# Loads of a Fourier-mixing kernel: 128 partitions in place of 112

## The chip, the cores and the metric

The kernel runs on one core of a Trainium2 chip. Five engines work beside each other: TensorE (PE, with its weight loads as PEld), VectorE (DVE), ScalarE (ACT), GpSimd (POOL) and SyncE (SP), which here only issues DMA transfers. Each engine takes its instructions in the order of the program and waits for others by semaphores. DRAM is reached through 16 DMA engines. The metric is device time in microseconds (us).

## What is computed

x has the shape (8, 3136, 256). Each batch is convolved circularly with a filter along its 3136 tokens, then mixed by a two-dimensional Fourier transform, and goes through a normalised two-layer product:

```
X = np.fft.rfft(x, axis=1);  Y = X * (filt_r + 1j * filt_i)
y = np.fft.irfft(Y, n=3136, axis=1)
u = y + np.real(np.fft.fft(np.fft.fft(y, axis=1), axis=2))
un = (u - mean(u)) / sqrt(var(u) + 1e-6)
out = u + np.maximum(un @ w_ch1, 0) @ w_ch2
```

## The kernel before

The transform over 3136 = 112 x 28 tokens is done in stages of small matrix products, which is why 112 rows stand in most tiles. For each of the eight batches a chain runs:

- `forward1`: seven loads of x, `[112, 4, 256]` in float32 each (448 KB), from the caller's array of the shape (8, 112, 28, 256). VectorE takes the largest magnitude of each tile (`absmax`, the tile `mx`), a power of two `sx` comes of the seven, then 14 steps each scale a piece, multiply it by the table `s1`, split it in two float16 halves (`ast`, four buffers) and write it to the DRAM scratch tensor `d1`. Batch 0 has its own version, `first_forward1`, which multiplies in float32 while x still arrives.
- `forward2`: seven loads `at` of `[112, 8, 256]` float16, from d1 in another order of rows (runs of 512 bytes), 448 KB each. Their products with the table `s2` are multiplied by the filter, folded into the ring `eo` for the second transform, turned round by DMA transposes (`z`; on PE in batch 0), multiplied by the table `i1` and written to a second scratch tensor, `d2`.
- `inverse2` (the batch's `back` part): seven loads `b` of d2, like those of d1, products with the table `i2`, and stores `ys` to a third tensor, `dy`.

Groups of 256 rows of dy are then fetched as `y`, mixed (`channels`), normalised (`un`, `u16`), turned by two DMA transposes into `ut`, and multiplied by both weights in eight parts: `first_product` (tile `h`, line 770; ScalarE and VectorE make its two halves in lines 779 and 780) and `second_product` (`acc`, line 799). These two products of the weights are the larger part of PE's work. Batch b + 1's chain is woven between the groups of batch b.

d1 and d2 are allocated anew for each batch from a pool with two buffers each. All tables are loaded once, s2 and i1 in chunks behind the at loads of batch 0.

What sets the order: the generators `there` and `back` are advanced step by step from a loop over PE's products, `after(...)` adds marks before which an instruction is not put, and a scheduler with a timeline of its own then sets the order on each engine. All DMAs stand in SP's one queue. They use eight semaphores in turn, so that a DMA is not issued before the one eight places ahead of it has landed.

The lines that matter, and the allocation of the scratch:

```
nc.sync.dma_start(xs[q], a["x"][b, :, 4 * q : 4 * q + 4])
d1v = d1.rearrange("(u r) n h c -> (r n h) u c", r=2)
last = nc.sync.dma_start(ats[ch], d1v[:, 8 * ch : 8 * ch + 8])
d1 = dp.tile([112, 28, 2, 256], F16, tag="d1", name=f"d1_{b}")
```

Of the kernel before, what the change touches and what calls it, by code (L numbers as in the profile page):

```python
# [9 lines left out]
F32 = mybir.dt.float32  # L10
F16 = mybir.dt.float16
# [13 lines left out]
C = 256  # L25
# [169 lines left out]
def _program(ctx, tc, nc, a, NB):  # L195
    cp = ctx.enter_context(tc.tile_pool(name="cp", bufs=1))
    xp = ctx.enter_context(tc.tile_pool(name="xp", bufs=7))
    fp = ctx.enter_context(tc.tile_pool(name="fp", bufs=2))
    mp = ctx.enter_context(tc.tile_pool(name="mp", bufs=2))
    tp = ctx.enter_context(tc.tile_pool(name="tp", bufs=2))  # L200
    dp = ctx.enter_context(tc.tile_pool(name="dp", bufs=2, space=DRAM))
# [4 lines left out]
    marks = {}  # L206
# [15 lines left out]

    s1 = cp.tile([112, 2, 112], F16, name="s1")
    s1f = fp.tile([112, 112], F32, tag="t2", name="s1f", bufs=2)
    s2 = cp.tile([112, 56, 2, 56], F16, name="s2")
    i1 = cp.tile([112, 28, 2, 112], F16, name="i1")
    i2 = cp.tile([112, 2, 2, 2, 64], F16, name="i2")
# [102 lines left out]

    def first_forward1(d1):

        xs = [xp.tile([112, 4, 256], F32, tag="big", name=f"x_0_{q}") for q in range(7)]
        m = tp.tile([112, 8], F32, tag="mx", name="mx_0")
        ps = {}

        def product(q):
            if q in (3, 4):
                p = ps_o.tile([128, 2, 256], F32, tag="pso", name=f"s1_0_{q}")[:112]
            else:  # L340
                p = bank(f"s1_0_{q}")[:112].rearrange("p (n c) -> p n c", c=256)
# [17 lines left out]
        yield  # L359
        for q in range(14):  # L360
            if q not in ps:
                product(q)
            p = ps.pop(q)
            st = fp.tile([112, 2, 2, 256], F16, tag="ast", name=f"ast_0_{q}", bufs=4)
            marks["act"] = nc.scalar.activation(st[:, :, 0], p, AF.Copy, scale=sx[:112, 1:2]).ins
            marks["dve", q] = nc.vector.scalar_tensor_tensor(
                st[:, :, 1], p, sx[:112, 1:2], st[:, :, 0], op0=ALU.mult, op1=ALU.subtract
            ).ins
            marks["d1", q] = nc.sync.dma_start(d1[:, 2 * q : 2 * q + 2], st).ins
            yield  # L370

    def forward1(b, d1):
        xs = [xp.tile([112, 4, 256], F32, tag="big", name=f"x_{b}_{q}") for q in range(7)]
        m = tp.tile([112, 8], F32, tag="mx", name=f"mx_{b}")
        for q in range(7 + XLAG):
            with after(("y", 1), ("un", 0)) if b == 1 else nullcontext():
                if q < 7:
                    with after("sp") if b > 1 else nullcontext():
                        nc.sync.dma_start(xs[q], a["x"][b, :, 4 * q : 4 * q + 4])
                if q >= XLAG:  # L380
                    with after("h"):
                        absmax(m[:, q - XLAG : q - XLAG + 1], xs[q - XLAG], AX.XY)
            if q < 6 + XLAG:
                yield
        nc.vector.tensor_reduce(m[:, 7:8], m[:, 0:7], axis=AX.X, op=ALU.max)
        row = pow2(m[:, 7:8], f"x{b}")
        sx = tp.tile([128, 2], F32, tag="sx", name=f"sx_{b}", bufs=3)
        spread(sx, row, f"x{b}")
        sxs[b] = sx
        yield  # L390
        for q in range(14):
            x = xs[q // 2][:, 2 * (q % 2) : 2 * (q % 2) + 2]
            x16 = fp.tile([112, 2, 2, 256], F16, tag="x16", name=f"x16_{b}_{q}", bufs=3)
            nc.scalar.activation(x16[:, 0], x, AF.Copy, scale=sx[:112, 1:2])  # L394
            nc.vector.scalar_tensor_tensor(
                x16[:, 1], x, sx[:112, 1:2], x16[:, 0], op0=ALU.mult, op1=ALU.subtract
            )
            p = bank(f"s1_{b}_{q}")[:112].rearrange("p (n c) -> p n c", c=256)
            for i, (hs, hx) in enumerate(((0, 0), (0, 1), (1, 0))):
                nc.tensor.matmul(p, s1[:, hs], x16[:, hx], start=i == 0, stop=i == 2)  # L400
            st = fp.tile([112, 2, 2, 256], F16, tag="ast", name=f"ast_{b}_{q}", bufs=4)
            nc.scalar.copy(st[:, :, 0], p)
            nc.vector.tensor_tensor(st[:, :, 1], p, st[:, :, 0], op=ALU.subtract)
            nc.sync.dma_start(d1[:, 2 * q : 2 * q + 2], st)
            yield

    def load_s2(ch):
        nc.sync.dma_start(s2[:, 8 * ch : 8 * ch + 8], a["c_s2"][:, 8 * ch : 8 * ch + 8])

    def load_i1(ch):  # L410
        nc.sync.dma_start(i1[:, 4 * ch : 4 * ch + 4], a["c_i1"][:, 4 * ch : 4 * ch + 4])

    def forward2(b, d1, d2):
        al = cp.tile([128, 3], F32, name=f"alpha_{b}")
# [94 lines left out]
        def inverse1(ch, h):  # L509
# [33 lines left out]
    def inverse2(b, d2):  # L543
        dy = dp.tile([2, NS, 256], F32, tag="dy", name=f"dy_{b}", bufs=3)
        dys[b] = dy
        d2v = d2.rearrange("(m r) j l c -> (r j l) m c", r=2)
        al = alphas[b]
        bts = {}

        def load(c):  # L550
            if c < 7:
                bts[c] = fp.tile([112, 4, 2, 256], F16, tag="b2", name=f"b2_{b}_{c}", bufs=2)
                with after("dy"):
                    marks["b", c] = marks["sp"] = nc.sync.dma_start(
                        bts[c].rearrange("p j h c -> p (j h) c"), d2v[:, 8 * c : 8 * c + 8]
                    ).ins

        def store(k, s, r, ys, c, j0):
# [383 lines left out]
    for r, f in enumerate(("frT", "fiT")):  # L942
        for h in range(4):
            part = slice(784 * (h % 2), 784 * (h % 2) + 784)
            nc.sync.dma_start(ft[:, r, h // 2, part], a[f][:, h // 2, part])
    nc.sync.dma_start(fnyq, a["frN"])
    for q in range(14):
        advance(9 + q)
        if q == 2:
            with after(("d1", 0)):  # L950
                nc.sync.dma_start(s2[:, :16], a["c_s2"][:, :16])
        for i in range(8):
            if FILTERS_AT[i] == q:
                measure_filters(i)
        weigh(9 + q)
# [40 lines left out]
def device_arrays(x, filt_r, filt_i, moe_w_ch1, moe_w_ch2):  # L996
# [22 lines left out]


# [27 lines left out]
```

## Time and profile before

| | |
|---|---|
| median of 3 runs | 1541.23 us |
| the three runs | 1541.23, 1531.26, 1541.39 us |
| span of the profiled execution, first to last instruction | 1534.0 us |
| PE busy in the span | 91% |
| HBM read, written | 113.36 MB, 102.76 MB |
| DMA packets' time on the hardware queue, share of 16 engines | 72.5% |

Of the profiled execution the page gives the span alone, not a time of the kind that the runs have.

A profile is one execution. Busy time of an engine is the time of its instructions; a wait is the idle time just before an instruction, put down to what came last before it ("DVE mx L267 <- DMA x<-x" is VectorE idle ahead of line 267, until an x load landed). A busy share averages over stages with different limits, so the stretches of the span are read one by one. The kernel's time is that of the chain that ends last; work on other engines counts only where that chain waits for it. Names like `at<-d` say what is written and what is read.

### The profile page before, as it was taken

How to read it: one execution, taken by the hardware profiler on the slowest of the kernel's cores; microseconds unless marked ns; L12 is line 12 of the kernel's file. 1: busy time of each engine (PE TensorE's matmuls, PEld its weight loads, DVE VectorE, ACT ScalarE, POOL GpSimd, SP SyncE). 2: the span in 40 equal slices, each digit the busy share in tenths (PEclk: the TensorE clock that was granted, in tenths of full speed). 3: DMA queues.
4: the chain of work that ended last, by engine and by line, in shares of the span. 5: the costliest groups of instructions: out<-in, count | busy, mean ns of one | idle time of the engine just before them, and what ended most of it. 6: DMA issues, size and time to landing. Idle time of an engine off the chain costs nothing.

```text
span 1534.0 us, 30300 instructions
## 1 busy us (share of the span) xinstructions
PE 1398.7 (91%) x11331; PEld 934.1 (61%) x11331; DVE 1092.8 (71%) x2388; ACT 771.3 (50%) x1426; POOL 539.9 (35%) x682
## 2 busy tenths in 40 slices
PE   5454899787999999999999999899999999999998
PEld 1432567454665677566765677566665667666666
DVE  5576878586967887687758877688767877565562
ACT  4466545354545464474544654374644655443341
POOL 3652049205810195006720284016620284110110
PEclk8675999998999999999999999999999999999999
DMA  8868478959985797859986796859876896644320
GB/s 263 218 205 219 101 163 176 219 157 206 203 216 146 175 227 174 208 152 214 192 192 161 192 231 159 211 146 220 183 189 158 195 237 144 166 107 110 95 55 29
DMA packets 429491, 268.98 MB, mean 175 GB/s; under 512 B 218624, under 2 KB 395824, under 8 KB 429344
## 3 DMA queue, kind: packets, MB, share of 16 engines
q1 hardware_dynamic: 429344, 267.05, 72.5%
q8 instruction: 89, 1.46, 0.4%
q14 instruction: 58, 0.48, 0.1%
HBM read 113.36 MB, written 102.76 MB: 141 GB/s over the span
## 4 chain that ended last, share of the span: by engine, by line
PE 67%; DMA 11%; DVE 7%; issue 3%; POOL 3%; ACT 2%; SPq 1%; DVEq 0%; POOLq 0%; ACTq 0%
PE h L770 26%; PE acc L799 26%; DMA x<-x 3%; PE s L400 3%; PE y L577 3%; DMA at<-d 2%; PE mix L646 2%; DVE y L656 2%; PE i L514 1%; DMA b<-d 1%; PE i L516 1%; PE i L515 1%; PE s L449 1%; DVE mx L267 1%; PE s L450 1%
## 5 line engine op out<-in xcount | busy, mean ns | idle before, releaser
L770 PE MATMUL h<-ut,w1s 128*128 128x512 f16 x2352 | 590.8, 385 | 24.6 <-DVE h L780 20.5
L799 PE MATMUL acc<-w2s,h 128*128 128x256 f16 x4704 | 599.9, 274 | 1.3 <-DVE h L780 1.3
L799 PEld LDWEIGHTS <-h 128*128 128x128 f16 x4704 | 456.4, 98 | 146.8 <-issue 13.6
L779 ACT ACTIVATE h<-h 128x512 f16<-128x512 f32 x392 | 233.1, 595 | 411.9 <-PE h L770 404.6
L780 DVE SCALAR_TENSOR_TENSOR h<-h,h 128x512 f16<-128x512 f32 x392 | 267.6, 683 | 200.3 <-ACT h L779 199.3
L741 POOL TENSOR_TENSOR u<-un,u 128x512 f16<-128x512 f32 x94 | 107.8, 1163 | 758.0 <-ACT u L739 745.6
L770 PEld LDWEIGHTS <-w1s 128*128 128x128 f16 x2352 | 223.8, 99 | 236.7 <-issue 48.1
L656 DVE SCALAR_TENSOR_TENSOR y<-mix,alpha,y 128x508 f32<-128x508 f32 (+1 forms) x368 | 156.0, 474 | 8.2 <-PE mix L646 6.9
L736 ACT ACTIVATE un<-y,sb 128x256 f32<-128x256 f32 x196 | 101.8, 589 | 44.0 <-DVE sb L729 38.8
L469 POOL TENSOR_TENSOR y<-yt,y 128x448 f16<-128x448 f32 x105 | 108.4, 1036 | 16.5 <-ACT y L468 16.2
L584 ACT ACTIVATE ys<-y,alpha 128x512 f32<-128x512 f32 x112 | 76.1, 686 | 71.4 <-PE y L577 71.0
L519 DVE TENSOR_TENSOR bt<-i,bt 112x512 f16<-112x512 f32 x112 | 75.7, 682 | 49.1 <-ACT bt L518 47.4
L267 DVE TENSOR_REDUCE mx<-x 112x1 f32<-112x1024 f32 x56 | 67.7, 1214 | 52.0 <-DMA x<-x 52.0
L463 POOL TENSOR_TENSOR yt<-yt,t 128x224 f32<-128x224 f32 x112 | 73.9, 660 | 81.9 <-DVE t L459 53.6
L455 DVE SCALAR_TENSOR_TENSOR yt<-s,pF,ft 128x448 f32<-128x448 f32 x112 | 75.3, 675 | 37.7 <-PE s L450 34.9
L449 PE MATMUL s<-s,at 112*128 112x56 f16 x896 | 62.7, 191 | 32.6 <-DMA at<-d 28.1
L400 PE MATMUL s<-x,s 112*112 112x512 f16 x294 | 87.3, 388 | 3.9 <-ACT x L394 1.9
L577 PE MATMUL y<-b,i 112*64 112x512 f16 (+1 forms) x480 | 74.1, 396 | 18.1 <-DMA b<-d 17.9
L518 ACT CAST bt<-i 112x512 f16<-112x512 f32 x112 | 64.9, 585 | 49.9 <-PE i L516 43.7
L808 DVE SCALAR_TENSOR_TENSOR y<-acc,beta,y 128x512 f32<-128x512 f32 x98 | 71.2, 742 | 25.7 <-PE acc L799 25.5
L468 ACT CAST y<-yt 128x448 f16<-128x448 f32 x112 | 62.6, 564 | 38.6 <-POOL yt L464 35.6
L449 PEld LDWEIGHTS <-at 112*128 112x128 f16 x896 | 55.8, 98 | 42.6 <-DMA at<-d 36.0
(133 smaller groups left out, 1663.4 us busy)
## 6 DMA issues: line engine op xcount, KB each, us to landing
x<-x SPq DMA_DIRECT2D x56, 448.0 KB
d<-ast SPq DMA_DIRECT2D x112, 224.0 KB
at<-d SPq DMA_DIRECT2D x56, 448.0 KB
d<-bt SPq DMA_DIRECT2D x112, 224.0 KB
b<-d SPq DMA_DIRECT2D x56, 448.0 KB
out<-y SPq DMA_DIRECT2D x98, 256.0 KB
y<-dy SPq DMA_DIRECT2D x92, 256.0 KB
dy<-ys SPq DMA_DIRECT2D x208, 112.0 KB
```

Source lines behind the costliest of these rows:

```text
L267: nc.vector.tensor_reduce(dst, src, axis=axis, op=ALU.max, apply_absolute_value=True)
L400: nc.tensor.matmul(p, s1[:, hs], x16[:, hx], start=i == 0, stop=i == 2)
L449: nc.tensor.matmul(o, w, s2[:, U, 0].rearrange("p (r k) -> p r k", r=2), start=True, stop=False)
L469: last = half(b, hf == 1).tensor_tensor(ylo, ytv, yhi, op=ALU.subtract)
L577: nc.tensor.matmul(p[64 * h : 64 * h + 64, js], i2[:, t, h, i], bt[:, o + js.start : o + js.stop, h], start=i == 0, stop=i == 1,)
L656: nc.vector.scalar_tensor_tensor(out, p, al, y, op0=ALU.mult, op1=ALU.add)
L736: nc.scalar.activation(un[:m, k], y[:m, t, k], AF.Identity, bias=sb[:m, i, 1:2], scale=sb[:m, i, 3:4])
L741: marks["u16", g] = low.tensor_tensor(u16[:m, :, :, 1], unv, u16[:m, :, :, 0], op=ALU.subtract).ins
L770: marks["pe"] = nc.tensor.matmul(p[:, c0 : c0 + n].rearrange("p (t k q) -> p t k q", k=2, q=m), w1s[:, d, hw, 128 * f : 128 * f + 128], ut ...
L779: nc.scalar.activation(h[:, 0, :nt], p[:, :nt], AF.Relu)
L780: marks["h"] = nc.vector.scalar_tensor_tensor(h[:, 1, :nt], p[:, :nt], 0.0, h[:, 0, :nt], op0=ALU.max, op1=ALU.subtract).ins
L799: nc.tensor.matmul(acc[:m, k], h[:, hh, c0 : c0 + m], w2s[:, f, hw], start=f == 0 and k == 0 and i == 0, stop=f == 7 and k == 1 and i == 2,)
```

## The change

Loads of x, of d1, of d2 and of the tables s2, i1 and i2 fill 128 partitions in place of 112. Compute instructions still use the first 112: `xs`, `ats`, `bts`, `s2`, `i1` and `i2` are now views `[:112]` of larger tiles, and the stores to d1 and d2 still have 112 rows. An SBUF tile takes as many bytes in each partition as before.

- x comes padded with 16 rows of zeros, as (8, 7, 128, 4, 256): each tile is one contiguous piece of 512 KB.
- The tables get 16 rows of zeros; a chunk of s2 or i1 grows from 196 to 224 KB.
- d1 and d2 get a 113th row, and there are two of each for the whole run (`scratch`, used by even and odd batches). A load reads 128 rows from the same start: the last 16 are the first rows of the next slot, and for the last slot the tail, which is filled with zeros once. Loads from d1 and d2 grow from 448 to 512 KB.

```diff
+    def rows128(d, u0, n):
+        v = d[:112].rearrange("(u r) n h c -> (r n h) u c", r=2)[:, u0 : u0 + n]
+        (row, _), *rest = v.ap
+        return bass.AP(tensor=v.tensor, offset=v.offset, ap=[[row, 128], *([s, m] for s, m in rest)])
...
-    s2 = cp.tile([112, 56, 2, 56], F16, name="s2")
+    s2_rows = cp.tile([128, 56, 2, 56], F16, name="s2")
+    s2 = s2_rows[:112]
...
-        xs = [xp.tile([112, 4, 256], F32, tag="big", name=f"x_{b}_{q}") for q in range(7)]
+        raw = [xp.tile([128, 4, 256], F32, tag="big", name=f"x_{b}_{q}") for q in range(7)]
+        xs = [t[:112] for t in raw]
...
-                        nc.sync.dma_start(xs[q], a["x"][b, :, 4 * q : 4 * q + 4])
+                        nc.sync.dma_start(raw[q], a["x"][b, q])
...
-            nc.sync.dma_start(d1[:, 2 * q : 2 * q + 2], st)
+            nc.sync.dma_start(d1[:112, 2 * q : 2 * q + 2], st)
...
-                ats[ch] = xp.tile([112, 8, 256], F16, tag="big", name=f"at_{b}_{ch}")
-                last = nc.sync.dma_start(ats[ch], d1v[:, 8 * ch : 8 * ch + 8])
+                at = xp.tile([128, 8, 256], F16, tag="big", name=f"at_{b}_{ch}")
+                ats[ch] = at[:112]
+                last = nc.sync.dma_start(at, rows128(d1, 8 * ch, 8))
...
-                bts[c] = fp.tile([112, 4, 2, 256], F16, tag="b2", name=f"b2_{b}_{c}", bufs=2)
+                bt = fp.tile([128, 4, 2, 256], F16, tag="b2", name=f"b2_{b}_{c}", bufs=2)
+                bts[c] = bt[:112]
...
-                        bts[c].rearrange("p j h c -> p (j h) c"), d2v[:, 8 * c : 8 * c + 8]
+                        bt.rearrange("p j h c -> p (j h) c"), rows128(d2, 8 * c, 8)
...
+    scratch = [
+        [dp.tile([113, 28, 2, 256], F16, tag=f"d{i}_{k}", name=f"d{i}_{k}", bufs=1) for i in (1, 2)] for k in range(2)
+    ]
+    zeros = fp.tile([16, 256], F16, tag="ef", name="zeros", bufs=1)
+    nc.vector.memset(zeros, 0.0)
+    def fill_tails():
+        for d1, d2 in scratch:
+            for d in (d1, d2):
+                nc.sync.dma_start(d[112, :8].rearrange("n h c -> (n h) c"), zeros)
...
-        d1 = dp.tile([112, 28, 2, 256], F16, tag="d1", name=f"d1_{b}")
-        d2s[b] = dp.tile([112, 28, 2, 256], F16, tag="d2", name=f"d2_{b}")
+        d1, d2s[b] = scratch[b % 2]
...
     nc.sync.dma_start(fnyq, a["frN"])
+    fill_tails()
```

The scheduler sees other transfers and sets the order anew; most of what moves are swaps of neighbours. Three places, before and after.

SP's queue in the opening, before: the last filter loads (`ft`), then the first writes of d1 (`d_0<-ast`) and the first part of s2 (`c_s`). In brackets stand the semaphores waited for, DMAHW0 to DMAHW7 in turn:

```order
L945 DMA ft<-fiT 128x784 [waits DMAHW0_49]
L946 DMA fnyq<-frN 128x2 [waits DMAHW1_49]
L369 DMA d_0_116<-ast_0_174 112x1024 [waits DMAHW2_49,DVE_49]
L951 DMA s_83<-c_s 112x1792 [waits DMAHW3_49]
L369 DMA d_0_116<-ast_1_184 112x1024 [waits DMAHW4_49,DVE_49]
L369 DMA d_0_116<-ast_2_194 112x1024 [waits DMAHW5_49,DVE_49]
```

SP's queue at the same place after, with the four fills of the tails (`zeros`):

```order
L967 DMA ft<-fiT 128x784 [waits DMAHW0_49]
L968 DMA fnyq<-frN 128x2 [waits DMAHW1_49]
L619 DMA d_0_115<-zeros 16x256 [waits DMAHW2_49,DVE_49]
L619 DMA d_0_116<-zeros 16x256 [waits DMAHW3_49]
L619 DMA d_1_117<-zeros 16x256 [waits DMAHW4_49]
L619 DMA d_1_118<-zeros 16x256 [waits DMAHW5_49]
L379 DMA d_0_115<-ast_0_182 112x1024 [waits DMAHW6_49,DVE_49]
L974 DMA s_83<-c_s 128x1792 [waits DMAHW7_49]
L379 DMA d_0_115<-ast_1_192 112x1024 [waits DMAHW0_49,DVE_49]
```

Every DMA behind the fills moved on by four semaphores: the first write of d1 waited for the second of the eight filter loads and now for the sixth.

SP's queue ahead of batch 2, before: writes of batch 1's d2, the transposes of group 5 (`ut_5`), then batch 1's first b load and batch 2's x loads:

```order
L746 DMA_TRANSPOSE ut_5_3111<-u16_5_0_3212 128x8x128
L520 DMA d2_1_1448<-bt_1_6_0_3035 112x1024
L520 DMA d2_1_1448<-bt_1_6_1_3046 112x1024
L746 DMA_TRANSPOSE ut_5_3111<-u16_5_1_3254 128x8x128
L554 DMA b2_1_0_3087<-d2_1_1448 112x8x256
L379 DMA x_2_0_3091<-x 112x1024
```

The same stretch of SP's queue after:

```order
L531 DMA d2_1_118<-bt_1_6_1_3052 112x1024
L565 DMA b2_1_0_3093<-d2_1_118 128x8x256
L390 DMA x_2_0_3095<-x 128x1024
L390 DMA x_2_1_3096<-x 128x1024
L390 DMA x_2_2_3097<-x 128x1024
L390 DMA x_2_3_3098<-x 128x1024
L390 DMA x_2_4_3099<-x 128x1024
L390 DMA x_2_5_3100<-x 128x1024
L565 DMA b2_1_1_3174<-d2_1_118 128x8x256
L768 DMA_TRANSPOSE ut_5_3115<-u16_5_0_3216 128x8x128
L768 DMA_TRANSPOSE ut_5_3115<-u16_5_1_3258 128x8x128
```

Both transposes moved behind six x loads and the second b load. On PE the products `h_5_0` that read `ut_5` moved too: 20 products of `acc` and the 8 of `y_1_2` and `y_1_3` that stood behind them now stand ahead.

VectorE's order in the same stretch, before: the maxima `mx_2` of batch 2's x tiles, between the second halves `h16` of the products (group, part):

```order
L267 TENSOR_REDUCE mx_2_3098<-x_2_3_3094 112x1
L267 TENSOR_REDUCE mx_2_3098<-x_2_4_3095 112x1
L780 SCALAR_TENSOR_TENSOR h16_4_6_3625<-h_4_6_3618,h16_4_6_3625 128x512
L267 TENSOR_REDUCE mx_2_3098<-x_2_5_3096 112x1
L780 SCALAR_TENSOR_TENSOR h16_4_7_3677<-h_4_7_3670,h16_4_7_3677 128x512
L780 SCALAR_TENSOR_TENSOR h16_5_0_3723<-h_5_0_3716,h16_5_0_3723 128x512
L267 TENSOR_REDUCE mx_2_3098<-x_2_6_3097 112x1
```

VectorE's order there after:

```order
L276 TENSOR_REDUCE mx_2_3102<-x_2_3_3098 112x1
L802 SCALAR_TENSOR_TENSOR h16_4_6_3629<-h_4_6_3622,h16_4_6_3629 128x512
L276 TENSOR_REDUCE mx_2_3102<-x_2_4_3099 112x1
L802 SCALAR_TENSOR_TENSOR h16_4_7_3681<-h_4_7_3674,h16_4_7_3681 128x512
L276 TENSOR_REDUCE mx_2_3102<-x_2_5_3100 112x1
L830 SCALAR_TENSOR_TENSOR y_4_2212<-acc_4_0_3393,beta_96,y_4_2212 128x512
L830 SCALAR_TENSOR_TENSOR y_4_2212<-acc_4_1_3394,beta_96,y_4_2212 128x512
L802 SCALAR_TENSOR_TENSOR h16_5_0_3727<-h_5_0_3720,h16_5_0_3727 128x512
L802 SCALAR_TENSOR_TENSOR h16_5_1_3768<-h_5_1_3761,h16_5_1_3768 128x512
L276 TENSOR_REDUCE mx_2_3102<-x_2_6_3101 112x1
```

One maximum less stands ahead of `h16_4_6` and of `h16_4_7`, and the seventh moved behind `h16_5_1`. In the later batches the maxima kept their places, or moved by a few.

More of the change, by code (lines that the diff above doesn't have):

```diff
@@ L224, in _program @@
     s1f = fp.tile([112, 112], F32, tag="t2", name="s1f", bufs=2)
-    s2 = cp.tile([112, 56, 2, 56], F16, name="s2")
-    i1 = cp.tile([112, 28, 2, 112], F16, name="i1")
-    i2 = cp.tile([112, 2, 2, 2, 64], F16, name="i2")
+    s2_rows = cp.tile([128, 56, 2, 56], F16, name="s2")
+    s2 = s2_rows[:112]
+    i1_rows = cp.tile([128, 28, 2, 112], F16, name="i1")
+    i1 = i1_rows[:112]
+    i2_rows = cp.tile([128, 2, 2, 2, 64], F16, name="i2")
+    i2 = i2_rows[:112]
     mix = cp.tile([128, 2, 320], F16, name="mix")
@@ L331, in first_forward1 @@
     def first_forward1(d1):
-        xs = [xp.tile([112, 4, 256], F32, tag="big", name=f"x_0_{q}") for q in range(7)]
+        raw = [xp.tile([128, 4, 256], F32, tag="big", name=f"x_0_{q}") for q in range(7)]
+        xs = [t[:112] for t in raw]
         m = tp.tile([112, 8], F32, tag="mx", name="mx_0")
@@ L345, in first_forward1 @@
         for q in range(7):
-            nc.sync.dma_start(xs[q], a["x"][0, :, 4 * q : 4 * q + 4])
+            nc.sync.dma_start(raw[q], a["x"][0, q])
             if q == 1:
@@ L368, in first_forward1 @@
             ).ins
-            marks["d1", q] = nc.sync.dma_start(d1[:, 2 * q : 2 * q + 2], st).ins
+            marks["d1", q] = nc.sync.dma_start(d1[:112, 2 * q : 2 * q + 2], st).ins
             yield
     def forward1(b, d1):
-        xs = [xp.tile([112, 4, 256], F32, tag="big", name=f"x_{b}_{q}") for q in range(7)]
+        raw = [xp.tile([128, 4, 256], F32, tag="big", name=f"x_{b}_{q}") for q in range(7)]
+        xs = [t[:112] for t in raw]
         m = tp.tile([112, 8], F32, tag="mx", name=f"mx_{b}")
@@ L403, in forward1 @@
             nc.vector.tensor_tensor(st[:, :, 1], p, st[:, :, 0], op=ALU.subtract)
-            nc.sync.dma_start(d1[:, 2 * q : 2 * q + 2], st)
+            nc.sync.dma_start(d1[:112, 2 * q : 2 * q + 2], st)
             yield
     def load_s2(ch):
-        nc.sync.dma_start(s2[:, 8 * ch : 8 * ch + 8], a["c_s2"][:, 8 * ch : 8 * ch + 8])
+        nc.sync.dma_start(s2_rows[:, 8 * ch : 8 * ch + 8], a["c_s2"][:, 8 * ch : 8 * ch + 8])
     def load_i1(ch):
-        nc.sync.dma_start(i1[:, 4 * ch : 4 * ch + 4], a["c_i1"][:, 4 * ch : 4 * ch + 4])
+        nc.sync.dma_start(i1_rows[:, 4 * ch : 4 * ch + 4], a["c_i1"][:, 4 * ch : 4 * ch + 4])
     def forward2(b, d1, d2):
@@ L431, in load @@
                         if ch == 6:
-                            nc.sync.dma_start(i2, a["c_i2"])
+                            nc.sync.dma_start(i2_rows, a["c_i2"])
                             nc.sync.dma_start(mix, a["c_mix"])
@@ L519, in inverse1 @@
             marks["low"] = nc.vector.tensor_tensor(bt[:, :, 1], p, bt[:, :, 0], op=ALU.subtract).ins
-            marks["bt", ch] = nc.sync.dma_start(d2[:, j : j + 2], bt).ins
+            marks["bt", ch] = nc.sync.dma_start(d2[:112, j : j + 2], bt).ins
         far = 3
@@ L545, in inverse2 @@
         dys[b] = dy
-        d2v = d2.rearrange("(m r) j l c -> (r j l) m c", r=2)
         al = alphas[b]
@@ L950, in _program @@
             with after(("d1", 0)):
-                nc.sync.dma_start(s2[:, :16], a["c_s2"][:, :16])
+                nc.sync.dma_start(s2_rows[:, :16], a["c_s2"][:, :16])
         for i in range(8):
@@ L1005, in device_arrays, with rows128 @@
     c = np.ascontiguousarray
+    def rows128(v, axis):
+        pad = [(0, 0)] * v.ndim
+        pad[axis] = (0, 128 - v.shape[axis])
+        return c(np.pad(v, pad))
     def words(w):
@@ L1010, in device_arrays @@
     return {
-        "x": c(x.reshape(nb, 112, 28, C)[..., perm]),
+        "x": rows128(x.reshape(nb, 112, 7, 4, C)[..., perm].transpose(0, 2, 1, 3, 4), 2),
         "frT": lay(filt_r),
@@ L1016, in device_arrays @@
         "w2": words(c(moe_w_ch2[:, perm].reshape(2, 4, 128, C).transpose(2, 0, 1, 3).reshape(128, 2, 1024))),
-        **constants(),
+        **{k: rows128(v, 0) if k in ("c_s2", "c_i1", "c_i2") else v for k, v in constants().items()},
     }
```

1 line of the change is left out of this document (removed).

## The prediction, made before the result

> **What bounds the kernel now.** I read the busy times first, then the stretches of the span, then who waits for whom, then single loads in the timeline.
>
> ```profile
> span 1534.0 us, 30300 instructions
> PE 1398.7 (91%) x11331; PEld 934.1 (61%) x11331; DVE 1092.8 (71%) x2388; ACT 771.3 (50%) x1426; POOL 539.9 (35%) x682
> ```
>
> The stretches show where the 135 us lie in which PE does not compute (columns: length, then busy us of PE, PEld, DVE, ACT and POOL, granted clock, DMA share, GB/s):
>
> ```profile
> core 0: us, PE busy (x) PEld busy (x) DVE busy (x) ACT busy (x) POOL busy (x), PEclk, DMA share, GB/s
> 0.00:50.00 50.00, 21.75 (x52) 8.38 (x53) 22.10 (x47) 15.70 (x31) 14.81 (x28) 0.77 0.88 266
> 50.00:100.00 50.00, 29.27 (x407) 26.63 (x403) 37.12 (x68) 31.98 (x51) 43.41 (x55) 0.77 0.76 205
> 100.00:150.00 50.00, 22.49 (x142) 12.32 (x143) 34.31 (x85) 32.41 (x65) 12.21 (x10) 0.57 0.81 205
> 150.00:200.00 50.00, 45.70 (x276) 27.53 (x275) 43.52 (x90) 29.90 (x55) 2.32 (x2) 0.93 0.43 114
> 200.00:1300.00 1100.00, 1049.95 (x8779) 705.24 (x8778) 837.49 (x1820) 573.31 (x1065) 445.66 (x569) 0.98 0.81 189
> 1300.00:1534.00 234.00, 229.55 (x1684) 153.95 (x1681) 118.30 (x282) 88.05 (x162) 21.48 (x19) 1.00 0.38 93
> ```
>
> The first 150 us hold 76.5 us of idle PE, with DMA at 0.76 to 0.88: batch 0 runs alone there. From 200 to 1300 PE is idle for 50.05 us, and the waits of that stretch name most of them (us in all, times, longest):
>
> ```profile
> ...
> DVE h L780 <- ACT h L779: 106.2, 101, 3.0
> ...
> DVE mx L267 <- DMA x<-x: 43.8, 21, 5.4
> ...
> PE h L770 <- DVE h L780: 20.5, 12, 4.1
> ...
> PE s L449 <- DMA at<-d: 17.6, 10, 10.4
> ```
>
> The waits for x and for `h` on VectorE belong together. VectorE takes the maximum of an x tile in its own order; while the tile is not there, the product's second half `h`, queued behind it, is late, and PE waits for that. The timeline of batch 6 (start, us, engine, line, then the idle time before and its releaser):
>
> ```profile
> 976.83 1.21 DVE L267 TENSOR_REDUCE mx<-x 112x1 f32<-112x1024 f32 x1
> 983.17 1.22 DVE L267 TENSOR_REDUCE mx<-x 112x1 f32<-112x1024 f32 x1 [5.13 <-DMA x<-x]
> ...
> 985.87 0.68 DVE L780 SCALAR_TENSOR_TENSOR h<-h,h 128x512 f16<-128x512 f32 x1
> ...
> 986.60 2.72 PE L770 MATMUL h<-ut,w1s 128*128 128x512 f16 x6 [4.10 <-DVE h L780]
> ```
>
> VectorE stood for 5.13 us, and PE for 4.10. So PE bounds the middle, with holes that loads from DRAM make; loads bound parts of the first 100 us.
>
> **The rate of a load, 112 rows against 128.** The only sizes that the change alters are rows and bytes of loads, so the sum rests on this. Opening, x tiles (first and last of four at even distance), then three stretches: only x in flight, only the 128-row filter loads, and the first at loads with 112-row tables:
>
> ```profile
> 11.16 1.22 DVE L267 TENSOR_REDUCE mx<-x 112x1 f32<-112x1024 f32 x1 [0.57 <-DMA x<-x]
> ...
> 16.55 1.22 DVE L267 TENSOR_REDUCE mx<-x 112x1 f32<-112x1024 f32 x1 [0.61 <-DMA x<-x]
> ```
>
> ```profile
> 7.00:15.00 8.00, 6.27 (x11) 2.04 (x10) 5.15 (x5) 0.00 (x0) 0.00 (x0) 1.00 1.04 259
> 18.00:24.00 6.00, 3.25 (x6) 1.65 (x7) 3.57 (x9) 2.42 (x4) 5.53 (x6) 0.50 1.04 396
> 47.00:49.00 2.00, 0.00 (x0) 0.00 (x0) 0.00 (x0) 0.00 (x0) 0.00 (x0) 0.50 1.12 258
> ```
>
> An x tile of 448 KB takes (16.55 - 11.16) / 3 = 1.80 us, at 259 GB/s. The filters, 128 rows of 3136 bytes, run at 396 GB/s, and in both stretches the engines are fully busy (share 1.04). So 112 rows use all engines' time and move two thirds of the bytes. At 396 GB/s the new x tile of 512 KB takes 1.32 us: 0.48 less, though it is larger, and still above the 1.22 us of its reduction.
>
> [...]
>
> For at and b, with rows of 512 bytes, no 128-row load exists in the trace. A lone b load, and the mixed stretch of at loads and tables:
>
> ```profile
> GB/s 123 68 34 20 68 82 68 157 218 246 287 335 362 348 362 328 348 362 335 362 335 328 328 307 294 266 280 294 259 205 150 205 232 280 280 287 280 280 280 273
> ```
>
> ```profile
> DMA packets 3620, 2.45 MB, mean 245 GB/s; under 512 B 124, under 2 KB 3618, under 8 KB 3618
> ```
>
> In the fortieths of 100 to 103 us a b load alone runs at about 345, and beside the next one at 280; the burst of at loads (47 to 57 us) at 245. With 128 rows I take the 345 of the load that nothing disturbs: at 448 KB / 245 = 1.87 us becomes 512 KB / 345 = 1.52, that is -0.35. Bounds: 2.14 (still 245, +0.27) and 1.32 (396, -0.55). A lone b load goes from 1.33 to 1.52, +0.19. A table of 196 KB at 245 (0.82) becomes 224 KB at 396 (0.58), -0.24.
>
> **The change part by part.**
>
> *x of batch 0.* Seven tiles in a row, each ending VectorE's wait: 7 x -0.48 = -3.3 us before the first scale is known. Bounds -3.3 and +1.8 (a seventh dearer, 7 x 0.26). The filter loads behind them move by the same time.
>
> *Tails.* Four writes of 8 KB and one memset. The memset lies beside the wait for the first x tile; its nearest row is the small memset below. On SP four issues at 0.3 to 0.4 us (the row of `d<-ast`) stand ahead of the first write of d1, and every DMA behind them waits for a semaphore four places later:
>
> ```profile
> 0.94 0.07 DVE L489 MEMSET es<- 128x2 f32 x2
> ```
>
> ```profile
> L369 SPq DMA_DIRECT2D d<-ast x14: 303/304/420, 21.7 to 38.9; - x14
> ```
>
> The first write of d1 then waits for the sixth filter load where it waited for the second, the second write for the eighth. Four `ast` buffers cover about 2 us of that, and the writes queue behind the filters' bytes anyway. I take 0; bounds 0 and +2. Without the cover, ScalarE's fifth `ast` would start later by that.
>
> *Tables and at of batch 0.* PE waits, from 0 to 50 us and from 50 to 100:
>
> ```profile
> PE s L449 <- DMA at<-d: 9.4, 1, 9.4
> ```
>
> ```profile
> PE s L449 <- DMA s<-c_s: 3.3, 2, 2.0
> ...
> PE s L449 <- DMA at<-d: 1.1, 1, 1.1
> ```
>
> One chunk (at, s2, i1) goes from 1.87 + 2 x 0.82 = 3.51 to 1.52 + 2 x 0.58 = 2.68 us. Of the 9.4 the last 0.35 goes; of the 4.4 I take a little over a third, since POOL is busy for 43.41 of these 50 us and is late next. Sum -2.0; bounds 0 and -4.8.
>
> *b.* Twice the chain of 98 to 112 us goes through a lone b load, +0.19 each: +0.4; bounds 0 and +1. (With -0.35 in later bursts nobody waits for b.)
>
> ```profile
> 98.74 4.04 DMA b<-d
> 107.69 4.23 DMA b<-d
> ...
> 209.26 5.88 DMA at<-d
> ...
> 353.40 5.30 DMA at<-d
> ```
>
> *x of batches 2 to 7.* 21 waits, 43.8 us of VectorE, 20.5 of PE. If each wait shrinks by one tile's 0.48, VectorE gains 10.1 us and PE 20.5 / 43.8 of it, 4.7. If in each of six batches the whole stream of seven counts, 6 x 3.3 = 20 us, more than half of which (13) can reach PE. The long waits stand at late tiles, so a little above the low end: -6.0; bounds -4.7 and -13, and +2.5 (21 x 0.26 x 0.47) if loads get dearer.
>
> *at of batches 1 to 7.* Ten waits, 17.6 us, one of them 10.4. Each goes down by at least the load's own 0.35; three at loads are issued together and disturb each other (the chain's 5.3 to 5.9 us from issue to landing, against 4.04 for the b load), so up to 1 us. -4.0; bounds -7 and +2.7.
>
> *The moved instructions.* Order changes by swaps of neighbours, all but the ones shown for batch 2: costed at 0, as a rival below.
>
> Sum: -3.3 + 0 - 2.0 + 0.4 - 6.0 - 4.0 = -14.9 us. The page gives no other time of the profiled execution than its span; 1534.0 - 14.9 = 1519.1. The median of the runs stands 7.2 us above that span (one of three stands 2.7 below it), so 1541.2 - 14.9 = 1526.3 us.
>
> **Rivals.**
>
> [...]
>
> *Hidden.* The loads are faster, but after 200 us the same holes come back from the next late work (ScalarE's `h` before VectorE's), as PE is busy for 95% there. Only -3.3 and -0.35 stay: 1537.6. For it: VectorE's `h` waits for ScalarE's 101 times, 106.2 us. Against it: the 5.13 us above end in a load and in nothing else.
>
> *The order.* In batch 2 both transposes of `ut_5` now stand behind six x loads and a b load, some 7 x 1.4 us of transfers; PE takes `h_5_0` late, too, with 20 products of `acc` and 8 of `y` ahead of it (some 3 us). I price what is left at 5 us: 1531.3. With the same in other batches it would be a loss.
>
> **How the numbers follow.** Forecast 0.66, hidden 0.13, order 0.13, dearer 0.08. A measurement of this kernel can tell about 1% (15.4 us) from no change. The forecast's centre lies just inside that, so 0.32 of its 0.66 is faster and 0.34 the same; order gives 0.03 faster, 0.07 same, 0.03 slower; hidden is the same; dearer 0.06 same, 0.02 slower. Together 0.35, 0.60, 0.05. The range: below, all upper bounds at once (-3.3 - 4.8 - 13 - 7 = -28) give 1513, rounded to 1512; above, to 1541, with the hidden case and most of the order's inside. Left out are the dearer loads, the order's worst and a tail, below 0.2.
>
> **What would show it.** Right: x tiles of the opening 1.3 us apart; sx some 3 us earlier; VectorE's wait for x after 200 us below 35 us and PE's for `h` below 16; PE's for at below 14. Wrong: x tiles 1.8 apart or more (dearer); waits for x gone but those of PE for `h` as before (hidden); PE waiting for `ut` near 300 us (order); d1's first writes late behind the tails.

## The result, and the profile after

| | before | after |
|---|---|---|
| median | 1531.42 us (6 runs) | 1508.52 us (6 runs) |
| lowest and highest run | 1529.21, 1541.39 | 1505.13, 1511.43 |
| ratio, 95% interval | | 0.9825 [0.9803, 0.9847] |
| span of the profiled execution | 1534.0 us | 1508.7 us |

The change makes the kernel 1.75% faster by the ratio (the two medians alone give 22.9 us, 1.5%), more than the 1% that can be told from nothing. The forecast had the side of the change right and its size too small: 1526.3 was said, and 1508.52 lies 3.5 us below the range. The 17.8 us between them have two parts, the base and the sum. By these runs 9.8 are the base: the three runs shown had a median of 1541.23, with three more it is 1531.42. The other 8.0 are the sum: -14.9 forecast, -22.9 measured (-25.3 in the spans of the two profiled executions). Six runs are few, though: in the four series below, the kernel before has medians of 1534.6 to 1536.4 us over 9 to 21 runs each. With 1535 some 6 us are the base and some 12 the sum (-26.5 measured).

Busy times after, from the page:

```profile
span 1508.7 us, 30305 instructions
PE 1393.7 (92%) x11331; PEld 934.7 (62%) x11331; DVE 1096.5 (73%) x2389; ACT 772.4 (51%) x1426; POOL 538.5 (36%) x682
```

PE does the same work. 20.3 of the 25.3 us are idle time of PE that is gone (135.3 to 115.0), the other 5.0 busy time of the same 11331 matmuls; the granted clock of 100 to 150 us, for one, rose from 0.57 to 0.65. The stretches after (columns as in the prediction; the first one holds x tiles and filters alone):

```profile
7.00:13.00 6.00, 5.42 (x11) 1.94 (x9) 5.40 (x5) 0.00 (x0) 0.00 (x0) 1.00 1.03 413
0.00:50.00 50.00, 23.50 (x70) 10.05 (x71) 24.20 (x53) 15.70 (x31) 15.42 (x29) 0.73 0.84 291
50.00:100.00 50.00, 30.33 (x388) 27.88 (x386) 40.17 (x68) 33.35 (x53) 42.26 (x55) 0.74 0.71 219
100.00:150.00 50.00, 26.81 (x184) 14.50 (x185) 35.53 (x92) 33.55 (x66) 11.27 (x9) 0.65 0.74 233
150.00:200.00 50.00, 46.73 (x298) 29.03 (x296) 44.13 (x97) 30.74 (x56) 2.44 (x2) 0.97 0.44 116
200.00:1280.00 1080.00, 1041.97 (x8759) 703.45 (x8757) 836.43 (x1806) 575.89 (x1070) 446.82 (x571) 0.99 0.80 200
```

In the opening the engines are as busy as before (share 1.03) and move 413 GB/s where they moved 259. From 200 us to the end of the last x stage PE is idle for 38.0 us, where it was 50.05 in the like stretch before. The waits there:

```profile
DVE h L802 <- ACT h L801: 106.0, 99, 3.0
...
DVE mx L276 <- DMA x<-x: 28.2, 15, 5.2
...
PE s L460 <- DMA at<-d: 17.1, 9, 10.7
...
PE h L792 <- DVE h L802: 7.9, 10, 2.2
```

VectorE's wait for x fell from 43.8 to 28.2 us, and PE's for `h` from 20.5 to 7.9. PE's wait for at did not move (17.6 to 17.1). VectorE's wait for ScalarE's `h` is as it was (106.2 to 106.0).

VectorE's maxima in the opening, after, then the scale `sx` after and before:

```profile
8.06 6.35 DVE L276 TENSOR_REDUCE mx<-x 112x1 f32<-112x1024 f32 x5 [0.41 <-DMA x<-x]
...
16.50 0.16 DVE L273 COPY sx<-pb_x 128x2 f32<-128x2 f32 x1 [0.67 <-PE pb_x L272]
```

```profile
19.96 0.16 DVE L264 COPY sx<-pb_x 128x2 f32<-128x2 f32 x1 [0.68 <-PE pb_x L263]
```

Five maxima in 6.35 us are 1.27 each, close behind each other: the reduction (1.22 us) and the load (512 KB at 413 GB/s are 1.27 us) now take about the same, and sx stands 3.5 us earlier.

At this point two things were open. The order on the engines had been set anew, and the waits for x had fallen by more than loads that are 0.48 us shorter explain. So: did the transfers save the time, or the order?

### The profile page after: what moved, and what is told of

Read it like the earlier page. It is cut to its first block, busy times and chain, and to the rows that moved or that the text cites. A ratio compares the mean times of both kernels' runs of the same rounds, so it can differ in the third digit from the quotient of the medians.

```text
span 1508.7 us, 30305 instructions
## 1 busy us (share of the span) xinstructions
PE 1393.7 (92%) x11331; PEld 934.7 (62%) x11331; DVE 1096.5 (73%) x2389; ACT 772.4 (51%) x1426; POOL 538.5 (36%) x682
## 3 DMA queue, kind: packets, MB, share of 16 engines
q8 instruction: 89, 1.46, 0.4%
## 4 chain that ended last, share of the span: by engine, by line
PE 64%; DMA 13%; DVE 7%; POOL 5%; issue 4%; SPq 3%; ACT 3%; DVEq 0%; POOLq 0%; ACTq 0%
PE h L792 25%; PE acc L821 25%; PE s L411 3%; DMA x<-x 3%; PE y L588 3%; DMA at<-d 3%; DMA d<-ast 2%; PE mix L668 2%; DVE y L678 2%; DVE mx L276 1%; PE i L525 1%; SPq L768 1%; PE i L527 1%; PE i L526 1%; PE s L460 1%
## 5 line engine op out<-in xcount | busy, mean ns | idle before, releaser
L792 PE MATMUL h<-ut,w1s 128*128 128x512 f16 x2352 | 583.6, 380 | 8.8 <-DVE h L802 8.3
L466 DVE SCALAR_TENSOR_TENSOR yt<-s,pF,ft 128x448 f32<-128x448 f32 x112 | 75.2, 674 | 35.2 <-PE s L461 30.4
L588 PE MATMUL y<-b,i 112*64 112x512 f16 (+1 forms) x480 | 75.2, 398 | 17.9 <-DMA b<-d 17.8
L414 DVE TENSOR_TENSOR ast<-s,ast 112x512 f16<-112x512 f32 x98 | 66.9, 683 | 20.9 <-ACT ast L413 20.2
```

Of the source, the lines that this page charges most:

```text
L588: nc.tensor.matmul(p[64 * h : 64 * h + 64, js], i2[:, t, h, i], bt[:, o + js.start : o + js.stop, h], start=i == 0, stop=i == 1,)
L792: marks["pe"] = nc.tensor.matmul(p[:, c0 : c0 + n].rearrange("p (t k q) -> p t k q", k=2, q=m), w1s[:, d, hw, 128 * f : 128 * f + 128], ut ...
```

## The experiments

Eight kernels split the change into transfers, order, x's layout, row counts and tails; four more move single rows of the order (a row is one instruction in an engine's queue). All ratios are against the kernel before, run on the same chip in the same series; the brackets are 95% intervals. A difference between two ratios is good to 0.2 to 0.4%, some 3 to 6 us.

### The order of the changed kernel, with loads of 112 rows again

To part transfers from order, loads are cut back after the scheduler has set the order, so that no instruction moves on any engine:

```diff
+    for block in nc.main_func.blocks:
+        for k, i in enumerate(block.instructions):
+            rows = ROWS.get(LOADS.get(i.name))
+            if rows:
+                block.instructions[k] = i.__replace__(ins=[cut(i.ins[0], rows)], outs=[cut(i.outs[0], rows)])
...
+ROWS = {"x": 112, "at": 112, "b": 112, "tables": 112}
```

All four kinds of load:

> The changed kernel with every instruction of every engine in its place, and the loads of x, at, b and the tables cut back to 112 rows after the order was set: tails, scratch tensors and x stored tile by tile stay. Theory T (a load of 128 rows is quicker, and that alone saves the time): the whole gain of about 25 us is gone, 1531 +- 4 us, x tiles of batch 0 land 1.8 us apart. Rival O (the order, set anew for the new sizes, saves it): the time stays near 1508, below 1515. Rival C (x now lies in one piece per tile, and that, not the row count, makes x quicker): x tiles still land 1.3 us apart with 112 rows, sx of batch 0 stays near 16.5 us, and about 14 us of the gain stay: near 1518.

Measured: 1518.03 us, ratio 0.9896 [0.9863, 0.9928]. With all loads at 112 rows 1.04 of the 1.75% stay. In the opening the x tiles come as slowly as before the change: the first and last of four maxima at even distance, and the stretch:

```profile
9.91 1.22 DVE L276 TENSOR_REDUCE mx<-x 112x1 f32<-112x1024 f32 x1 [2.04 <-DMA x<-x]
...
15.31 1.22 DVE L276 TENSOR_REDUCE mx<-x 112x1 f32<-112x1024 f32 x1 [0.58 <-DMA x<-x]
...
```

```profile
7.00:13.00 6.00, 6.00 (x11) 2.11 (x9) 3.31 (x3) 0.00 (x0) 0.00 (x0) 1.00 1.03 261
```

1.80 us a tile and 261 GB/s, though x now lies in one piece for each tile. So the layout (rival C) is not what makes x quicker; the number of rows is. That the time is the 1518 which C named is luck: its mechanism is not there. Theory T is wrong about the whole, and O is right about more than half.

The loads of x alone:

> The changed kernel in its own order with the loads of x alone cut back to 112 rows. T: the 3.5 us of the opening and the 14.2 us by which the stalls between y and sx of batches 2 to 7 became shorter come back: 1508 + 18 = 1526 (1522 to 1528). O: 1508 +- 3. C: 1508 +- 3 with x tiles still 1.3 us apart.

Measured: 1518.88 us, 0.9876 [0.9846, 0.9907]. Against the changed kernel's 0.9825 that is 0.5%, some 8 us, where T said 18 and O nothing.

The loads of at and b alone:

> The changed kernel in its own order with the loads of at and b alone cut back to 112 rows. T: what the x loads do not explain, the 6.5 us in batch 1 and part of the 4.4 us between 100 and 150 us, comes back: 1508 + 8 = 1516 (1512 to 1519). O: 1508 +- 3, those 11 us being the work of the order. The prediction's term for at of batches 1 to 7 (4.0 us through PE's wait for at) has already fallen: that wait went from 17.6 to 17.1 us only, so PE's wait for at should not grow by more than 2 us here.

Measured: 1515.49 us, 0.9865 [0.9843, 0.9887]: 0.4%, some 6 us, within what T said. PE's wait for at after 200 us is 19.6 us, 2.5 more than in the changed kernel and a little more than was expected; with all loads cut back it is 17.5.

The tables alone:

> The changed kernel in its own order with the loads of the tables (c_s2, c_i1, c_i2) alone cut back to 112 rows. T: seven pairs of table loads between 24 and 60 us, each about 0.25 us slower: 1508 + 0 to 2. O: 1508 +- 2.

Measured: 1510.09 us, 0.9833 [0.9809, 0.9857]. The tables are worth nothing that can be told apart.

### The order set for 112 rows

> The changed kernel's source with all loads of 112 rows, its order set for these sizes: tails, scratch tensors and x stored tile by tile stay. Against the kernel before its order differs at 74 places on PE; the changed kernel's differs at 204. In its own order with the loads cut back the changed kernel kept 1.0 per cent (ratio 0.990). Theory R (the order, set anew for the new sizes, keeps that 1.0 per cent): here it is gone, ratio 0.996 or more. Rival L (x in one piece per tile, or the scratch tensors that live throughout, keep it, whatever the order): ratio near 0.990, and DVE's wait for x after 200 us falls from 43.8 us as it did there. Rival N (the places at which the order moved are so many that any new order comes out better or worse by some us): in between.

Its edit: each load names 112 rows in the source, so the scheduler sees them.

```diff
-            nc.sync.dma_start(raw[q], a["x"][0, q])
+            nc.sync.dma_start(xs[q], a["x"][0, q, :112])
...
-                last = nc.sync.dma_start(at, rows128(d1, 8 * ch, 8))
+                last = nc.sync.dma_start(ats[ch], rows128(d1, 8 * ch, 8)[:112])
```

Measured: 1542.39 us, 1.0039 [1.0024, 1.0054]. With the same transfers, tails and layout as the first of these kernels (all loads cut back to 112 rows), the other order is 1.4% slower. Rival L falls, R holds. Nobody had asked the scheduler for the better order: whether it follows from the new sizes or came by chance, no run shows.

The same order with the loads stretched to 128 rows after it was set:

> The kernel with 112 rows and its own order, as above, with the loads of x and the tables, and of at and b but for the seventh of each batch, stretched to 128 rows after the order was set; no instruction moves, and the seventh loads of at and b keep 112 rows. If order and transfers add up, this gains against the kernel with 112 rows what the changed kernel gains in its order, 1518.0 - 1508.5 = 8 to 10 us, mostly in the opening (sx of batch 0 3.5 us earlier) and in the stalls before sx of batches 2 to 7. If the transfers alone do it, the ratio is near 0.983; if the order alone does it, nothing changes against the kernel with 112 rows.

Measured: 1530.24 us, 0.9968 [0.9954, 0.9982]. The four corners, as ratios against the kernel before (in the upper right one the seventh loads of at and b still have 112 rows):

| | loads of 112 rows | loads of 128 rows |
|---|---|---|
| order set for 112 rows | 1.0039 | 0.9968 |
| order of the changed kernel | 0.9896 | 0.9825 |

The transfers save 0.71% in either order (some 11 us), and the changed order 1.43% with either transfers (some 22 us against the order set for 112 rows; 16 us, or 1.04%, against the order of the kernel before). The two add up within the intervals.

PE's wait for `h` after 200 us parts the same way. With the order set for 112 rows it is 18.7 us with loads of 112 rows and 18.4 with 128, although VectorE's wait for x falls there from 45.2 to 35.2. With the changed order it is 10.2 and 7.9. So this wait goes mostly by the order, and little by the loads. The changed order with 112 rows:

```profile
PE h L792 <- DVE h L802: 10.2, 11, 2.7
...
DVE mx L276 <- DMA x<-x: 32.4, 16, 5.6
```

### Which row of the order

Where the two orders part with the same loads of 112 rows, batch 2 shows it best. VectorE with the order set for 112 rows, then PE:

```profile
306.53 1.22 DVE L276 TENSOR_REDUCE mx<-x 112x1 f32<-112x1024 f32 x1 [5.23 <-DMA x<-x]
307.66 0.68 DVE L802 SCALAR_TENSOR_TENSOR h<-h,h 128x512 f16<-128x512 f32 x1
```

```profile
308.40 0.81 PE L792 MATMUL h<-ut,w1s 128*128 128x512 f16 x3 [3.46 <-DVE h L802]
```

VectorE with the changed kernel's order:

```profile
299.67 0.69 DVE L802 SCALAR_TENSOR_TENSOR h<-h,h 128x512 f16<-128x512 f32 x1 [2.94 <-ACT h L801]
300.97 0.69 DVE L802 SCALAR_TENSOR_TENSOR h<-h,h 128x512 f16<-128x512 f32 x1 [0.60 <-ACT h L801]
304.74 1.22 DVE L276 TENSOR_REDUCE mx<-x 112x1 f32<-112x1024 f32 x1 [3.08 <-DMA x<-x]
```

In both VectorE waits for the seventh tile of x. In the first the `h` rows stand behind that wait, and PE loses 3.46 us; in the second two `h` rows stand ahead of it, and PE goes on. From 300 to 320 us PE was busy for 16.54 us at a granted clock of 0.85 in the first kernel, and for 19.34 us at 1.00 in the second:

```profile
300.00:320.00 20.00, 16.54 (x87) 9.67 (x86) 8.50 (x20) 5.34 (x9) 0.00 (x0) 0.85 0.59 160
```

```profile
300.00:320.00 20.00, 19.34 (x125) 11.93 (x124) 10.44 (x24) 9.03 (x16) 0.00 (x0) 1.00 0.54 162
```

Not all of that is the hole's: in the first kernel the clock is at half from 296.0 to 302.8 us, ahead of the hole, and again from 309.6 to 313.0, right behind it (0.90 over 280 to 300 us, 0.85 over 300 to 320); from 320 to 340 us it is the second kernel that has the lower clock (0.86 against 1.00). Over the whole span PE is idle for 135.5 us in the first kernel and 125.3 in the second, and busy for 1399.1 and 1391.0 with the same 11331 matmuls.

In batches 3 and 5 the changed kernel also has the seventh maximum behind one more `h` row, in batch 4 behind more rows of `y`. So the next kernels move that row alone, with the semaphore counts that hang on VectorE's place following it. First the cure, in the order for 112 rows (VectorE in batch 2):

```diff
-L276 TENSOR_REDUCE mx_3102<-x_6_3101 112x1
 L802 SCALAR_TENSOR_TENSOR h_5_0_3727<-h_0_3720,h_5_0_3727 128x512
 L830 SCALAR_TENSOR_TENSOR y_2212<-acc_1_3394,beta,y_2212 128x512
+L802 SCALAR_TENSOR_TENSOR h_5_1_3768<-h_1_3761,h_5_1_3768 128x512
+L276 TENSOR_REDUCE mx_3102<-x_6_3101 112x1
 L396 TENSOR_REDUCE mx_3102<-mx_3102 112x1
-L802 SCALAR_TENSOR_TENSOR h_5_1_3768<-h_1_3761,h_5_1_3768 128x512
```

> The kernel with 112 rows in its own order (ratio 1.004), every instruction in its place but six on DVE: in each of batches 2 to 7 the seventh maximum, which waits for the last tile of x, moves back to just ahead of the reduce over the seven (in batch 2 both move behind one more h row, as in the changed kernel). Loads, tails and the orders of PE, ACT, POOL and SP stay. Theory M (the order of the changed kernel saves its 1.4 per cent by the place of this one row: DVE no longer stands waiting for x in front of h rows that PE needs): the ratio falls from 1.004 to 0.990 +- 0.003, PE's wait for h after 200 us from 18.7 to about 10 us, DVE's wait for x from 45 to about 33. Rival P (the 190 moved places on PE, and those on ACT, POOL and SP, save it): the ratio stays at 1.000 or more.

Measured: 1532.2 us, 0.9972 [0.9947, 0.9997]. Half of the 1.4% (0.67%) is there, half is not; neither theory has the whole. PE's wait for `h` and VectorE's for x after 200 us, in the order for 112 rows and with the rows moved:

```profile
PE h L792 <- DVE h L802: 18.7, 8, 3.6
...
DVE mx L276 <- DMA x<-x: 45.2, 21, 6.3
```

```profile
PE h L792 <- DVE h L802: 14.1, 7, 5.0
...
DVE mx L276 <- DMA x<-x: 36.2, 15, 6.0
```

Then the reverse, in the changed kernel: the seventh maximum moved ahead in batches 2 to 5 (batch 2 shown).

```diff
 L276 TENSOR_REDUCE mx_3102<-x_5_3100 112x1
+L276 TENSOR_REDUCE mx_3102<-x_6_3101 112x1
 L830 SCALAR_TENSOR_TENSOR y_2212<-acc_0_3393,beta,y_2212 128x512
 L830 SCALAR_TENSOR_TENSOR y_2212<-acc_1_3394,beta,y_2212 128x512
 L802 SCALAR_TENSOR_TENSOR h_5_0_3727<-h_0_3720,h_5_0_3727 128x512
 L802 SCALAR_TENSOR_TENSOR h_5_1_3768<-h_1_3761,h_5_1_3768 128x512
-L276 TENSOR_REDUCE mx_3102<-x_6_3101 112x1
```

> The changed kernel (ratio 0.9825) with four rows moved on DVE alone: in batches 2 to 5 the seventh maximum moves ahead to just behind the sixth, past one to three h rows and some rows of y; nothing else moves, all loads keep 128 rows. Theory M: most of the 1.4 per cent is lost, ratio 0.992 to 1.000, PE's wait for h after 200 us back from 7.9 to 16 us or more. Rival P: ratio 0.986 or less.

Measured: 1523.13 us, 0.9916 [0.9888, 0.9944]. Four rows moved on one engine lose 0.9%, with every load at 128 rows. PE's waits there after 200 us:

```profile
PE h L792 <- DVE h L802: 10.7, 9, 4.3
PE acc L821 <- DVE y L830: 6.6, 2, 6.0
```

The loss is just short of what M expected (0.992 or more), and more than P allowed. PE's wait for `h`, which M put at 16 us or more, grew only from 7.9 to 10.7; another part of the loss shows as a wait of `acc` for the rows of `y` that now stood behind the maximum.

In the order for 112 rows the moved maxima gained nothing in batch 2 itself. ScalarE stood there at the copy `keep`, which waits for y from DRAM (line 719), with `h` rows behind it; the changed kernel has it two `h` rows later:

```profile
309.31 0.40 ACT L719 COPY keep<-y 1x256 f32<-1x256 f32 x1 [5.02 <-DMA y<-dy]
```

```diff
-L719 COPY keep_3512<-y_3199 1x256
 L801 ACTIVATE h_5_1_3768<-h_1_3761 128x512
 L801 ACTIVATE h_5_2_3794<-h_2_3787 128x512
+L719 COPY keep_3512<-y_3199 1x256
```

> The kernel with 112 rows and the six moved maxima (ratio 0.997, against 1.004 without them and 0.990 in the changed kernel's order), and with one row moved on ScalarE: in batch 2 the copy keep, which waits for y fetched from DRAM, moves behind the next two h rows, to where the changed kernel has it. The moved maxima gained nothing in batch 2 itself: there ScalarE stood 5.0 us at keep, and PE's acc waited 3.4 us for ScalarE's h behind it. Theory M2 (what is left of the order's gain lies in a second row of the same kind, this one): that wait of acc is gone, batch 2 ends 4 to 10 us earlier (PE's first product over b of batch 2 at 440 to 446 in place of 450.1), and the ratio falls to 0.990 to 0.994. Rival P2 (the rest lies in the places moved on PE): the ratio stays at 0.996 or more, batch 2 ends near 450.

Measured: 1530.38 us, 0.9977 [0.9956, 0.9998]: no gain in the time. In place it did what it should: PE's wait of `acc` for ScalarE fell from 3.4 to 0.6 us, and batch 2's first product over b came at 446.5 us after 450.1. But PE now waited 3.0 us for the maximum in its own row for the scale (`pt_x`), which the changed kernel has more than one `h` product later, and of the 3.6 us won in batch 2 2.1 were left at batch 7's first product over b, less than the runs can tell. So the second half of the order's gain is not in this row alone. Most of what is left lies in batch 2 again: this trace is 7.2 us behind the changed order with 112 rows at the first product over b of batch 2 (446.5 and 439.3), and 11.9 at that of batch 7. What is left lies in other rows of the order, on PE, SP or elsewhere, and was not taken apart.

### Row counts

```diff
+ROWS = {"x": 120}
```

> The changed kernel in its own order, with x loaded to 120 rows. What makes 112 rows slow: 260 ns for a packet of 4096 bytes where 128 rows take 159. [...] If the rate grows with the rows alone, packets take near 210 ns and the tiles are 1.5 us apart or more. If anything short of 128 rows is slow, near 260 ns and 1.8 us or more.

Measured: 1541.81 us, 1.0039 [1.0018, 1.0061], 2.1% above the changed kernel and slower than x with 112 rows. The maxima of the opening (first and last of four):

```profile
12.62 1.22 DVE L276 TENSOR_REDUCE mx<-x 112x1 f32<-112x1024 f32 x1 [0.96 <-DMA x<-x]
...
19.21 1.22 DVE L276 TENSOR_REDUCE mx<-x 112x1 f32<-112x1024 f32 x1 [1.03 <-DMA x<-x]
```

(19.21 - 12.62) / 3 = 2.20 us a tile, for 480 KB. From 7 to 15 us this kernel moves 238 GB/s; with x at 112 rows the kernel before, `n_x` and `n_all` move 259, 255 and 261 from 7 to 13 us, the changed kernel with 128 rows 413. So the rate does not grow with the rows from 112 to 120, and both counts short of 128 that were run are slow, as the last case said. Nor is it settled that 120 rows are slower by the byte than 112: one kernel with 120 rows was run.

### The tails, and the maxima moved in the changed kernel

```diff
+    all_scratch = dp.tile([4, 113, 28, 2, 256], F16, tag="d", name="d", bufs=1)
+    scratch = [[all_scratch[2 * k + i] for i in range(2)] for k in range(2)]
...
+        nc.sync.dma_start(all_scratch[:, 112, :8].rearrange("k n h c -> k (n h) c"), zeros)
```

> The changed kernel with the two pairs of scratch tensors in one, so that one DMA fills the four tails in place of four; every other instruction of every engine stays in its place. In the changed kernel SP issues the four fills 1 us apart, and the first write of d1 stands behind them, 2.67 us after sx of batch 0 where it stood 1.69 before. If that cost what the opening lost (3.5 us at sx, 2.1 at the first product over at), 1 to 1.4 us come back: first write of d1 near 18.2, first product over at near 46, 1507.5. Rival: the writes of d1 or the tables behind them set that time anyway, and nothing changes.

Measured: 1507.56 us, 0.9826 [0.9802, 0.985]: the same as with four fills. The writes of d1, after and with one fill:

```profile
L379 SPq DMA_DIRECT2D d<-ast x14: 303/304/385, 19.2 to 36.5; - x14
```

```profile
L379 SPq DMA_DIRECT2D d<-ast x14: 303/304/411, 18.3 to 35.9; - x14
```

The first write moves 0.9 us ahead, the last 0.6, and the first product over at 0.5 (47.09 to 46.56 us). Four fills in place of one cost nothing that the runs can tell; an effect of 1 us, which is what was at issue, is below what they resolve, and a kernel without any fill was not run.

That kernel with the seventh maximum further back:

> The changed kernel with one fill for the four tails (ratio 0.9826 alone), and with the seventh maximum of batches 2 to 7 moved back to just ahead of the reduce, past one or two rows in most batches; nothing else moves. Theory M: what is left of PE's wait for h after 200 us (8.2 us) falls to 5 or less, and the time by 2 to 6 us, ratio 0.979 to 0.982. Rival: where x has landed by then the reduce only comes later by the 1.2 us of the maximum itself, and the time stays, ratio 0.982 to 0.985.

Measured: 1502.86 us, 0.979 [0.976, 0.9821], the lowest median of all. The waits did what M said (PE's for `h` 8.2 to 4.1 us, VectorE's for x 28.7 to 23.6):

```profile
PE h L789 <- DVE h L799: 4.1, 5, 1.6
...
DVE mx L276 <- DMA x<-x: 23.6, 11, 5.1
```

Its interval overlaps with that of the changed kernel, so that it beats it is likely and not settled.

## Why the prediction fell short

**The step that failed** is "The moved instructions. Order changes by swaps of neighbours, all but the ones shown for batch 2: costed at 0". The order was worth some -16 us against the kernel before (0.9896 with all loads at 112 rows), by these runs more than all transfers together (some -11). The rows for it had been shown: VectorE's seventh maximum behind `h16_5_1`, and the 4.10 us that PE lost in batch 6 to just such a wait. They were read as what shorter loads would shrink, not as something that two places in a queue decide: PE's wait for `h` shrinks little with the loads (18.7 to 18.4 us in the order set for 112 rows) and nearly halves with the order (18.7 to 10.2, at 112 rows). Moving that row alone, in batches 2 to 7, gives back half of what the two orders differ by; which rows hold the other half stays open. The rival on the order was named with the wrong sign, for `ut_5` behind the x loads: PE's wait for `ut` after 200 us is 0.6 us after and was 3.2 before.

**The base** was a second, smaller miss: "The median of the runs stands 7.2 us above that span". In every later run that was profiled, the time of the profiled execution stands 1.7 to 2.0 us above its own span. So most of the 7.2 was the spread of three runs. On a base of 1535 the same sum gives 1520, and the same lower bound 1507, just below what was measured.

**The signs** that were to show the prediction right came out for x and `h` (28.2 us, below 35; 7.9, below 16), but not by the mechanism named. With 128 rows and the order set for 112 rows they are 35.2 and 18.4. That is near the sign of the hidden case: the waits for x shrink, those of PE for `h` stay. But the time still falls there, by 0.71%, so the hidden case does not hold either.

**x of batch 0**, -3.3: right. 413 GB/s, 1.27 us a tile, sx 3.5 us earlier. The terms for dearer loads (+1.8 here, +2.5 for batches 2 to 7) and their chance of 0.08 took a seventh more time for a seventh more bytes, 0.26 us on a tile of 1.80. No run shows such a term: a tile took 1.27 us with 128 rows where it took 1.80 with 112, at the same share of the engines' time (1.03 and 1.04).

**x of batches 2 to 7**, -6.0: about the right size as a share of the transfers, by another path. x in all gave some 8 us (0.9876 against 0.9825) where the two terms made 9.3. But PE's wait for `h`, through which the term was to come, is 8.6 us with x cut back to 112 rows and 7.9 without. Which wait the gain came through is open. The larger fall of the waits for x, 43.8 to 28.2, was mostly the order's: with 112 rows in the changed order it is already 32.4.

**at of batches 1 to 7**, -4.0, **tables and at of batch 0**, -2.0, and **b**, +0.4: -5.6 in all; at and b gave some 6 us (0.9865 against 0.9825) and the tables nothing that can be told. The size came out, the path did not: PE's wait for at after 200 us, which should have fallen below 14, stayed at 17.1 and is 17.5 to 19.6 with 112 rows. Its one long part, 10.7 us in batch 2, is 10.6 with 112 rows, so it is not the load's rate. In the changed kernel batch 2's last three writes of d1 are issued from 335.7 to 339.8 us, its first at loads at 343.06, and PE's first product over at comes at 348.0; the author's reading is that this chain makes the wait.

**Tails**, 0: nothing was seen against it. **All transfers together**: -14.9 forecast, some -11 measured. Taken one by one they make 15; the intervals allow both. With the order unchanged the sum would have promised some 4 us too much, in place of 8 to 12 too little.

Not settled: why the changed sources with 112 rows in their own order are 0.4% slower than the kernel before. The order differs at 74 places on PE, all in the first three batches. On VectorE batch 2's seventh maximum stands ahead of the first `h` row of group 5, where the kernel before has it behind that row, and it is there that PE loses the 3.46 us. That is a likely cause; no run parts it from the rest.

## What to carry to other kernels

When a change alters what a scheduler sees, the new order is a term of the sum and not a side effect: list the rows that wait for a transfer, and count what stands behind them on that engine before and after. A row that waits for DRAM belongs behind the work that others need soon, and one such row in each of four batches was worth as much here as the transfers' own rate (0.9% and 0.71%). To part the two, set the order with one size and run it with the other.

## What the hardware showed

- In the opening, loads of x into 128 partitions ran at 413 GB/s (the changed kernel), into 112 at 255 to 261 (the kernel before, `n_x`, `n_all`) and into 120 at 238 (`n_x120`), with all engines' time used in each case (share 1.02 to 1.05). The packets of 4096 bytes of batch 0's x took 159 ns at the median with 128 rows (the changed kernel) and 254 with 112 (the kernel before). For 120 rows share and rate make some 281 ns for 4096 bytes (1.02 x 16 x 4096 bytes / 238 GB/s), an estimate.
- The writes of d1 and d2 from 112 partitions took by the byte about as long as the 128-row loads: their packets of 2048 bytes took 84 ns at the median in both kernels, where 4096 bytes of x took 159 at 128 rows.
- In the kernel before, the six products behind the 4.10 us hole of batch 6 took 2.72 us, at a granted clock of 0.50 (986.3 to 989.7 us); the six at 990.70, at 1.00, took 1.46, which is 1.26 less. The clock was 1.00 ahead of the hole (980.0 to 982.5 us) and went to 0.50 near its end; what set it no run shows.
- The changed order was worth 1.4% of this kernel, and moving four of VectorE's 2389 instructions 0.9%.
